# Decays of the later blocks by two scans on 96 partitions, factor products moved ahead of the first value products, x of pair 1 moved to the weights' queue, and units reordered around the value products of pair 1

**Chip, cores, metric.** One core of a Trainium2 chip. The metric is the device time of one execution in microseconds (us). A profiled run has a span a little shorter than its time (128.0 for 129.73 us). "State" is fast or slow: a run more than 1.5% above the fastest of the same kernel counts as slow. Comparisons of times below use fast runs.

## The reference

A state-space scan (batch 4, 8 heads, 768 steps, head size 32, state size 16), then a bilinear layer with two weights of 256x1536 and one of 1536x256:

```python
for c in range(nc):                       # chunks of the sequence
    L = np.exp(cum[:, :, :, None] - cum[:, :, None, :]) * causal
    M = np.einsum('bhin,bhjn->bhij', Cc, Bc) * L
    y[:, :, sl] = np.einsum('bhij,bhjd->bhid', M, xc) + y_inter   # y_inter from state and C
    state = decay_full * state + np.sum(Bx, axis=2)
...
x = attn_out.transpose(0, 2, 1, 3).reshape(B * S, H * D)
return (x @ w_a) * (x @ w_b) @ w_out
```

## The kernel before

The kernel takes blocks of 128 steps, and each block in two pairs of batches: 12 pairs, numbered 0 to 11. For a pair, B and C are multiplied by factors from the running products of `a` (bm, cm), transposed on TensorE, and multiplied with each other (`scores`). The scores are masked and multiplied with x (`pv`, the value products). Six `unit`s then form the bilinear product hk of the pair, and two `out_half`s the output. TensorE has enough to do from pair 2 on; the head of the program, where everything first has to arrive, is what the change is about. Cuts are marked.

```python
    nc.sync.dma_start(a_sb, a.rearrange("b h (k q) -> (b h) k q", q=Q))      # 32 partitions
    # ... B, C, x of pair 0 by ScalarE and SyncE; B and C of pair 1 by SyncE
    load1(nc.sync, 1, 2, 0)               # x of pair 1
    load1(nc.sync, 1, 2, 1)
    load(2)
    # ... GpSimd: selections; load_w(0); causal
    load_w(1, (0,))                       # Wa chunk 1 (Wb chunk 1 follows behind the masks of pair 0)

    def scan(lo, hi):
        for k in range(lo, hi):
            nc.vector.tensor_tensor_scan(Pr[:, k], a_sb[:, k], zero, 1.0, ALU.mult, ALU.add)
    # ...
    scan(0, 1); sel_over_mid(0, 1); v = factors_mm(0, 1)
    # ... factors, bm and cm of pair 0 on DVE, scan(1, 2), transposes(0), scan(2, 3), scores(0), masks
    load_w(1, (1,))                       # Wb chunk 1
    load_w(2)
    scale_bc(1, 1, nc.gpsimd)             # cm, bm of pair 1
    scale_bc(1, 0, nc.gpsimd)
    # ... value products of pair 0
    scan(3, NBLK)
    h = unit(0, 0)
    turn(0)
    sel_over_mid(1, NBLK)
    h()
    go((0, 1))
    v = factors_mm(1, NBLK)               # 40 matmuls
    # ... hr, hs, hsx on DVE
    transposes(1, None, nc.vector.tensor_copy)
    nc.scalar.copy(flat(fC, 1, NBLK), v)
    h = unit(0, 2)
    fb(1)
    scores(1)                             # start: mark S of the prediction
    # ... masks of pair 1, unit (0, 3), G matmul
    go((0, 4))
    pv(1)                                 # start: mark P
    state(0)
    state(1)
    go((0, 5), (1, 0), (1, 1), (1, 2))
    transposes(2)
    go((1, 3))
    # ... scores(2), units (1, 4), (1, 5), out_half(0, 0), pv(2), out_half(0, 1)
    transposes(3)
```

## Time and profile before

| | before |
|---|---|
| time, median of the first 3 runs | 131.09 us (130.17 to 131.13) |
| span, mean granted clock of the profiled run | 128.0 us, 0.999 |
| TensorE busy | 93% |

The prediction shows the page's rows, the windows, the waits and the chain of this kernel. Two views more are needed later. The view of transfers (destination and source, queue, size, median time from issue to landing):

```profile
a_sb<-in_a_dram SPq DMA_DIRECT2D x1, 96.0 KB, 2.1
cn<-in_C_dram ACTq DMA_DIRECT2D x1, 64.0 KB, 3.2
```

All decays arrived in 2.1 us, and the first half of C of pair 0 in 3.2. And TensorE's timeline (start, duration, line, operation, and in brackets the idle time before it with what ended it):

```profile
10.82 0.80 PE L476 MATMUL aps<-X2T,Wa 128*128 128x256 f16 x4
...
13.21 1.38 PE L225 MATMUL fps<-selr,Pr 32*64 32x16 f32 x40
...
31.51 0.28 PE L313 MATMUL SC<-ident,bm 128*128 128x128 f16 x2
```

Unit (0,0) starts at 10.82, the 40 factor matmuls stand on the path at 13.21, and the transposes of pair 3 start at 31.51. From there on TensorE is full, so the start of that last line, called T3 below, says what the head costs.

### The profile page before, as it was taken

What the parts mean: (1) busy time and instruction counts of PE and PEld (TensorE: products, weight loads), DVE (VectorE), ACT (ScalarE), POOL (GpSimd) and SP (SyncE); (2) the same over time, 40 slices, a digit from 0 to 9 for tenths busy, and PEclk for the clock granted to TensorE, in tenths of its full rate; (3) what the DMA queues carried; (4) which work ended last, traced back from release to release, by engine and by line L of the source; (5) the groups of instructions that cost most, each with busy time, mean ns of one, the idle gap of its engine ahead of it and who ended that gap; (6) DMA issues with size and microseconds to landing.
All of it is one profiled execution on the core that took longest, in us unless ns stands there. A gap on an engine that the chain in (4) does not pass through costs nothing.

```text
span 128.0 us, 4399 instructions
## 1 busy us (share of the span) xinstructions
PE 118.6 (93%) x1761; PEld 97.1 (76%) x1761; DVE 89.6 (70%) x178; ACT 66.5 (52%) x129; POOL 62.0 (48%) x106
## 2 busy tenths in 40 slices
PE   6969979799999999999999999999999999999960
PEld 2425757688887888888888888888888888888840
DVE  4676769658695976967958959959759569364420
ACT  3344567594836545455556456465445464564410
POOL 7966830799982925907828447338339100000000
PEclk9999999999999999999999999999999999999999
DMA  3999999775435666566456555565565310211203
GB/s 66 158 215 164 211 199 216 117 136 111 105 67 88 156 90 111 120 110 142 91 96 146 104 87 131 111 111 123 101 133 116 73 42 0 46 41 23 51 8 82
DMA packets 51555, 13.76 MB, mean 107 GB/s; under 512 B 45328, under 2 KB 51504, under 8 KB 51536
## 3 DMA queue, kind: packets, MB, share of 16 engines
q1 hardware_dynamic: 46560, 10.72, 43.8%
q0 software_dynamic: 3184, 2.36, 12.5%
q10 hardware_dynamic: 1792, 0.41, 1.6%
q8 instruction: 13, 0.21, 0.7%
q14 instruction: 6, 0.05, 0.1%
HBM read 11.13 MB, written 3.15 MB: 111 GB/s over the span
## 4 chain that ended last, share of the span: by engine, by line
PE 77%; DMA 9%; SPq 7%; POOL 1%; issue 1%; ACTq 1%; DVE 0%; POOLq 0%
PE ops L493 25%; PE aps L476 22%; PE bps L476 21%; DMA cn<-in_C_dram 9%; SPq L123 7%; PE SC L380 3%; PE SC L336 3%; PE SC L397 2%; ACTq L123 1%; POOL bm L262 1%; PE SC L313 0%; POOL cm L262 0%; DVE osb L506 0%; POOLq L451 0%; POOLq L262 0%
## 5 line engine op out<-in xcount | busy, mean ns | idle before, releaser
L486 DVE TENSOR_TENSOR hk<-bps,asb 128x512 f16<-128x512 f32 x72 | 49.2, 687 | 20.8 <-ACT asb L485 18.9
L485 ACT COPY asb<-aps 128x512 f32<-128x512 f32 x72 | 42.1, 587 | 17.9 <-PE aps L476 16.4
L476 PE MATMUL bps<-X2T,Wb 128*128 128x256 f16 x288 | 43.2, 273 | 1.1 <-ACT G L611 1.1
L476 PE MATMUL aps<-X2T,Wa 128*128 128x256 f16 x288 | 43.5, 273 | 0.1
L493 PE MATMUL ops<-Wo,hk 128*128 128x256 f16 x288 | 35.3, 273 | 0.0
L476 PEld LDWEIGHTS <-Wb 128*128 128x128 f16 x288 | 28.1, 98 | 4.5 <-issue 0.6
L493 PEld LDWEIGHTS <-hk 128*128 128x128 f16 x288 | 27.4, 98 | 4.1
L476 PEld LDWEIGHTS <-Wa 128*128 128x128 f16 x288 | 26.8, 98 | 4.8 <-issue 0.3
L370 DVE TENSOR_TENSOR t<-SC,causal 128x512 f16<-128x512 f32 x45 | 29.4, 681 | 1.3 <-ACT tmp L367 1.0
L451 POOL TENSOR_TENSOR sbd<-U,maskbd 128x512 f16<-128x512 f32 x10 | 11.5, 1154 | 21.1 <-DVE U L447 21.0
L508 ACT ACTIVATE osb<-ops 128x256 f32<-128x256 f32 x23 | 8.8, 383 | 23.6 <-PE ops L493 22.9
L249 POOL TENSOR_SCALAR x<-xn 128x512 f16<-128x512 f32 x9 | 13.4, 1489 | 0.8 <-DMA xn<-in_x_dram 0.2
L408 ACT ACTIVATE X2T<-SC 128x512 f16<-128x512 f32 x11 | 6.6, 597 | 5.1 <-PE SC L380 5.1
L262 POOL TENSOR_TENSOR bc<-cn,fC 128x128 f16<-128x128 f32 x16 | 6.1, 402 | 5.6 <-DMA cn<-in_C_dram 3.4
L262 POOL TENSOR_TENSOR t<-bn,fB 128x256 f16<-128x256 f32 x12 | 7.7, 639 | 0.1
L262 POOL TENSOR_TENSOR bc<-bn,fB 128x128 f16<-128x128 f32 x16 | 6.1, 401 | 0.0
L380 PEld LDWEIGHTS <-x 64*32 64x32 f16 x384 | 3.2, 91 | 3.2 <-ACT x L247 1.6
L201 PE MATMUL SC<-warm 128*128 128x512 f16 (+1 forms) x14 | 4.4, 453 | 1.2 <-DVE warm L150 1.2
L427 DVE STREAM_TRANSPOSE dt<-SC 128x64 f32<-128x64 f32 x9 | 2.2, 249 | 4.1 <-ACT X2T L408 4.1
L262 POOL TENSOR_TENSOR cm<-cn,fC 128x128 f16<-128x128 f32 (+1 forms) x5 | 2.1, 445 | 5.9 <-DMA cn<-in_C_dram 5.9
L368 POOL TENSOR_TENSOR t<-tmp,causal 128x512 f16<-128x512 f32 x3 | 3.5, 1156 | 3.1 <-ACT tmp L367 3.1
L380 PE MATMUL SC<-t,x 64*32 64x144 f16 (+1 forms) x352 | 4.8, 224 | 0.0
(69 smaller groups left out, 66.8 us busy)
## 6 DMA issues: line engine op xcount, KB each, us to landing
xn<-in_x_dram SPq DMA_DIRECT2D x23, 128.0 KB, 3.2
out_dram<-osb SPq DMA_DIRECT2D x46, 64.0 KB, 2.1
bn<-in_B_dram SPq DMA_DIRECT2D x23, 64.0 KB, 2.7
cn<-in_C_dram SPq DMA_DIRECT2D x23, 64.0 KB, 3.3
Wa<-in_moe_w_a_dram POOLq DMA_DIRECT2D x3, 256.0 KB, 6.8
Wb<-in_moe_w_b_dram POOLq DMA_DIRECT2D x3, 256.0 KB, 6.6
Wo<-in_moe_w_out_dram POOLq DMA_DIRECT2D x1, 768.0 KB, 10.2
xn<-in_x_dram ACTq DMA_DIRECT2D x1, 128.0 KB, 5.4
```

Source lines behind the costliest of these rows:

```text
L123: return eng.dma_start(pair_in[p][which][64 * bt : 64 * bt + 64].rearrange("i h r n -> i h (r n)"), src.rearrange("h (i r) n -> i h (r n)" ...
L249: eng.tensor_scalar(xo, xi, XS, None, ALU.mult)
L262: return eng.tensor_tensor(out=out, in0=i0, in1=i1, op=ALU.mult)
L370: nc.vector.tensor_tensor(out=o_, in0=i_, in1=c_, op=ALU.mult)
L380: nc.tensor.matmul(py[bt][32 * g : 32 * g + 32, u * (Q + N) : u * (Q + N) + w], s["X16"][k, h, r, :], s["T1"][k, h, r, 0:w], start=(first ...
L408: nc.scalar.activation(out=X2T[:, p].rearrange("p u t q -> p t u q"), in_=s["PY"][:, :, :, 0:Q], func=AF.Copy, scale=YS / XS,)
L451: nc.gpsimd.tensor_tensor(out=Sbd.rearrange("p t (h d) -> p t h d", h=H), in0=U32[:, p].unsqueeze(2).broadcast_to((128, 2, H, D)), in1=mas ...
L476: nc.tensor.matmul(ps[:, kk * 2 * Q : (kk + 1) * 2 * Q], W[:, f, k * 128 : (k + 1) * 128], X2T[:, p, f].rearrange("p t q -> p (t q)"), sta ...
L485: nc.scalar.copy(asb, a_ps)
L486: return lambda: nc.vector.tensor_tensor(out=s["hk"][:, 2 * k2 : 2 * k2 + 2, :].rearrange("p k q -> p (k q)"), in0=b_ps, in1=asb, op=ALU.mult)
L493: nc.tensor.matmul(o_ps[:, 0:d_model], hk[:, k, bt * Q : (bt + 1) * Q], Wo[:, k, :], start=(k == 0), stop=(k == NK - 1), skip_group_check= ...
L508: nc.scalar.activation(out=o_sb, in_=o_ps[:, 0:d_model], func=AF.Copy, scale=1.0 / (YS * YS))
```

## The change

The intent: scan block 0 alone from a small load, so that the head starts early; bring the other decays to 96 partitions (32 rows of batch and head, times three thirds of the sequence), so that two scans replace five; do the factor matmuls in TensorE's idle time before the first value products; leave SyncE's queue to B and C by giving x of pair 1 to GpSimd's; and reorder the units around the value products of pair 1.

```diff
-    nc.sync.dma_start(a_sb, a.rearrange("b h (k q) -> (b h) k q", q=Q))
+    nc.sync.dma_start(a0_sb, a.rearrange("b h s -> (b h) s")[:, 0:Q])
+    nc.gpsimd.dma_start(a_sb.rearrange("p t q -> p (t q)"), a.rearrange("b h (k c) -> k (b h) c", k=KP))
...
-    load1(nc.sync, 1, 2, 0)
-    load1(nc.sync, 1, 2, 1)
     load(2)
...
     load_w(0)
...
-    load_w(1, (0,))
+    load_w(1)
...
+    for t in range(2):
+        scan(Pr[:, t], a_sb[:, t])
+    nc.vector.reciprocal(rmid, Pr[:, :, 63])
...
     scores(0)
+    load1(nc.gpsimd, 1, 2, 0)
     n0 = tail(0, nc.gpsimd)
+    for t in range(2):
+        over_mid(nc.gpsimd, selr[:, t].rearrange("p k b t h -> p (k b t h)"), rmid[:, t : t + 1])
...
-    load_w(1, (1,))
+    load1(nc.gpsimd, 1, 2, 1)
     load_w(2)
-    scale_bc(1, 1, nc.gpsimd)
     scale_bc(1, 0, nc.gpsimd)
...
-    warmup(5, tcp)
...
+    warmup(1, tcp)
+    for t in range(2):
+        factors_mm([F[:, :, t, r] for r in range(2)], Pr[:, t], [selr[:, t, :, :, bt] for bt in range(2)])
+    nc.scalar.copy(flat(fC, 1, NBLK), fps[:, 2 * NBP * H : NBLK * 2 * NBP * H])
+    warmup(1, tcp)
...
     h = unit(0, 0)
     turn(0)
-    sel_over_mid(1, NBLK)
     h()
+    scale_bc(1, 1, nc.vector)
     go((0, 1))
-    v = factors_mm(1, NBLK)
...
-    go((0, 4))
     pv(1)
+    turn(1)
+    go((1, 0))
+    gps = bank("gps")          # the G matmul, on 96 rows
...
-    go((0, 5), (1, 0), (1, 1), (1, 2))
+    go((1, 2), (1, 3))
     transposes(2)
-    go((1, 3))
-    h = unit(1, 4)
+    go((0, 4))
+    h = unit(0, 5)
...
```

More of the change, by code (lines that the diff above doesn't have):

```diff
@@ L52 @@
     NG = NBLK - 1
+    KP = NBLK // 2
+    KR = KP * BH
     j = np.arange(128)
-    bh = np.arange(BH)
-    p32 = np.zeros((BH, 128 + nb * NG), np.float32)
-    p32[:, 0:128] = (bh[:, None] % H) == (j // N % 2 * (H // 2) + j // (2 * N))[None, :]
+    row = np.arange(KR)
+    p96 = np.zeros((KR, 128 + nb * KP), np.float32)
+    p96[:, 0:128] = (row[:, None] % H) == (j // N % 2 * (H // 2) + j // (2 * N))[None, :]
     for b in range(nb):
-        p32[b * H : (b + 1) * H, 128 + b * NG : 128 + (b + 1) * NG] = 1.0
-    p32_t = nc.inline_tensor(p32, "p32")
+        for k in range(KP):
+            p96[k * BH + b * H : k * BH + (b + 1) * H, 128 + b * KP + k] = 1.0
+    p96_t = nc.inline_tensor(p96, "p96")
     const = ctx.enter_context(tc.tile_pool(name="const", bufs=1))
-    c32 = const.tile([BH, p32.shape[1]], f32, name="c32")
+    c96 = const.tile([KR, p96.shape[1]], f32, name="c96")
     headm = const.tile([128, H], f32, name="headm")
@@ L68 @@
     causal = const.tile([128, 2, Q], f16, name="causal")
-    sel = const.tile([BH, 2, NBP, H], f32, name="sel")
-    indm = c32[:, 0:128]
-    selb = c32[:, 128 : 128 + nb * NG]
+    indm = c96[:, 0:128]
+    selb = c96[:, 128 : 128 + nb * KP]
     big = ctx.enter_context(tc.tile_pool(name="big", bufs=1))
-    a_sb = big.tile([BH, NBLK, Q], f32, name="a_sb")
-    zero = big.tile([BH, Q], f32, name="zero")
+    a_sb = big.tile([KR, 2, Q], f32, name="a_sb")
+    a0_sb = big.tile([BH, Q], f32, name="a0_sb")
+    zero = big.tile([KR, Q], f32, name="zero")
+    Pr0 = big.tile([BH, Q], f32, name="Pr0")
+    rmid0 = big.tile([BH, 1], f32, name="rmid0")
+    selr0 = big.tile([BH, NBP, 2, H], f32, name="selr0")
     Wa = big.tile([128, 2, d_ff], f16, name="Wa")
@@ L83 @@
     warm = big.tile([128, 512], f16, name="warm")
-    Pr = big.tile([BH, NBLK, Q], f32, name="Pr")
-    rmid = big.tile([BH, NBLK], f32, name="rmid")
-    selr = big.tile([BH, NBLK, 2, NBP * H], f32, name="selr")
+    Pr = big.tile([KR, 2, Q], f32, name="Pr")
+    rmid = big.tile([KR, 2], f32, name="rmid")
+    selr = big.tile([KR, 2, KP, NBP, 2, H], f32, name="selr")
     fB = big.tile([128, NBLK, 2, NBP, H], f32, name="fB")
     fC = big.tile([128, NBLK, 2, NBP, H], f32, name="fC")
-    hr = big.tile([BH, NG], f32, name="hr")
-    hs = big.tile([BH, NG], f32, name="hs")
-    hsx = big.tile([BH, nb, NG], f32, name="hsx")
-    G = big.tile([128, nb, NG], f32, name="G")
+    nxt = big.tile([KR, 2], f32, name="nxt")
+    hr = big.tile([KR, 2], f32, name="hr")
+    hs = big.tile([KR, 2], f32, name="hs")
+    hsx = big.tile([KR, nb, KP, 2], f32, name="hsx")
+    G = big.tile([128, nb, NBLK], f32, name="G")
     bc = [big.tile([128, 6, H, N], f16, name=f"bc{i}") for i in range(2)]
@@ L140 @@
     load1(nc.scalar, 0, 2, 1)
-    nc.scalar.dma_start(c32, p32_t.ap())
+    nc.scalar.dma_start(c96, p96_t.ap())
     load1(nc.sync, 0, 2, 0)
@@ L146 @@
     load1(nc.sync, 1, 1, 0)
-    load1(nc.sync, 1, 2, 0)
-    load1(nc.sync, 1, 2, 1)
     load(2)
     nc.vector.memset(warm.bitcast(u32), 0)
+    nc.vector.memset(ident, 1.0)
+    nc.vector.memset(headm, 1.0)
     nc.vector.memset(zero, 0.0)
-    for t_ in bc:
-        nc.vector.memset(t_[:, 0:4].rearrange("p k h n -> p (k h n)").bitcast(u32), 0)
-    nc.gpsimd.memset(sel, 1.0)
+    nc.vector.memset(causal, 1.0)
     nc.gpsimd.affine_select(
-        out=sel,
-        in_=sel,
-        compare_op=ALU.is_equal,
-        fill=0.0,
-        base=0,
-        pattern=[[-H, 2], [-2 * H, NBP], [-1, H]],
-        channel_multiplier=1,
+        out=ident, in_=ident, compare_op=ALU.is_equal, fill=0.0, base=0, pattern=[[-1, 128]], channel_multiplier=1
     )
-    nc.gpsimd.memset(headm, 1.0)
     for sign, base in ((1, 0), (-1, N - 1)):
@@ L177 @@
     )
-    nc.gpsimd.memset(ident, 1.0)
-    nc.gpsimd.affine_select(
-        out=ident, in_=ident, compare_op=ALU.is_equal, fill=0.0, base=0, pattern=[[-1, 128]], channel_multiplier=1
-    )
     KC = 4 * 128
@@ L190 @@
     load_w(0)
-    nc.gpsimd.memset(causal, 1.0)
     for bt in range(2):
@@ L203, in warmup, with scan, over_mid, factors_mm @@
             )
-    def scan(lo, hi):
-        for k in range(lo, hi):
-            nc.vector.tensor_tensor_scan(Pr[:, k], a_sb[:, k], zero, 1.0, ALU.mult, ALU.add)
-    def sel_over_mid(lo, hi):
-        nc.vector.reciprocal(rmid[:, lo:hi], Pr[:, lo:hi, 63])
-        nc.vector.tensor_tensor(
-            out=selr[:, lo:hi].rearrange("p k t c -> p k (t c)"),
-            in0=sel.rearrange("p t b h -> p (t b h)").unsqueeze(1).broadcast_to((BH, hi - lo, 2 * NBP * H)),
-            in1=rmid[:, lo:hi].unsqueeze(2).broadcast_to((BH, hi - lo, 2 * NBP * H)),
-            op=ALU.mult,
-        )
-    def factors_mm(lo, hi):
-        fps = psf.tile([128, 512], f32, name="fps", tag="ff")
-        F = fps[:, 0 : (hi - lo) * 2 * NBP * H].rearrange("p (k r c) -> p k r c", k=hi - lo, r=2)
-        for k in range(lo, hi):
-            for r in range(2):
-                for bt in range(2):
-                    nc.tensor.matmul(
-                        F[64 * bt : 64 * bt + 64, k - lo, r],
-                        Pr[:, k].rearrange("p (i r) -> p r i", r=2)[:, r],
-                        selr[:, k, bt],
-                        start=True,
-                        stop=True,
-                        skip_group_check=True,
-                        tile_position=(0, 64 * bt),
-                    )
-        return F.rearrange("p k r c -> p (k r c)")
+    def scan(pr, a_):
+        nc.vector.tensor_tensor_scan(pr, a_, zero[0 : pr.shape[0]], 1.0, ALU.mult, ALU.add)
+    def over_mid(eng, sr, rm):
+        n = rm.shape[0]
+        eng.tensor_scalar(sr, ident[0:n, 0:n], rm, None, ALU.mult)
+    def factors_mm(F, pr, sr):
+        for r in range(2):
+            for bt in range(2):
+                nc.tensor.matmul(
+                    F[r][64 * bt : 64 * bt + 64],
+                    pr.rearrange("p (i r) -> p r i", r=2)[:, r],
+                    sr[bt],
+                    start=True,
+                    stop=True,
+                    skip_group_check=True,
+                    tile_position=(0, 64 * bt),
+                )
     def flat(f, lo, hi):
@@ L535 @@
     warmup(1, SC[3], 128)
-    scan(0, 1)
-    sel_over_mid(0, 1)
-    v = factors_mm(0, 1)
+    scan(Pr0, a0_sb)
+    nc.vector.reciprocal(rmid0, Pr0[:, 63:64])
+    over_mid(nc.vector, selr0.rearrange("p b t h -> p (b t h)"), rmid0)
+    v = bank("fps")[:, 0 : 2 * NBP * H]
+    v5 = v.rearrange("p (r b h) -> p r b h", r=2, b=NBP)
+    factors_mm([v5[:, r] for r in range(2)], Pr0, [selr0[:, :, bt] for bt in range(2)])
     nc.vector.reciprocal(flat(fB, 0, 1), v)
@@ L544 @@
     n1 = scale_bc(0, 1, nc.vector)
-    scan(1, 2)
     tb, tcp = bank("tb"), bank("tc")
-    transposes(0, [tb, tcp], nc.vector.tensor_copy, lambda: warmup(2, SC[3], 128))
-    scan(2, 3)
+    transposes(0, [tb, tcp], None, lambda: warmup(2, SC[3], 128))
+    for t in range(2):
+        scan(Pr[:, t], a_sb[:, t])
+    nc.vector.reciprocal(rmid, Pr[:, :, 63])
     warmup(1, SC[3])
@@ L565 @@
     nc.gpsimd.tensor_copy(maskbd, headm.unsqueeze(2).broadcast_to((128, H, D)))
+    for t_ in bc:
+        nc.gpsimd.memset(t_[:, 0:4].rearrange("p k h n -> p (k h n)").bitcast(u32), 0)
     n0 = load(3)
     tc.add_manual_dep(n0[0].ins, wd[5].ins.name, AFTER, reason="weights first")
-    warmup(5, tcp)
+    fps = bank("fps")
+    F = fps[:, 0 : NBLK * 2 * NBP * H].rearrange("p (k t r b h) -> p k t r b h", k=KP, t=2, r=2, b=NBP)
+    warmup(1, tcp)
[3 more added lines that the diff above has]
+    warmup(1, tcp)
     py = st[0]["py"] = [bank("py0"), bank("py1")]
@@ L579 @@
     warmup(1, tcp, 128)
-    scan(3, NBLK)
     h = unit(0, 0)
     turn(0)
-    sel_over_mid(1, NBLK)
     h()
+    scale_bc(1, 1, nc.vector)
     go((0, 1))
-    v = factors_mm(1, NBLK)
-    nc.vector.tensor_tensor(out=hr, in0=Pr[:, 0:NG, Q - 1], in1=rmid[:, 0:NG], op=ALU.mult)
-    nc.vector.tensor_tensor(out=hs, in0=hr, in1=Pr[:, 1:NBLK, 63], op=ALU.mult)
-    nc.vector.tensor_tensor(
-        out=hsx,
-        in0=hs.unsqueeze(1).broadcast_to((BH, nb, NG)),
-        in1=selb.rearrange("p (b g) -> p b g", b=nb),
-        op=ALU.mult,
-    )
     transposes(1, None, nc.vector.tensor_copy)
-    nc.scalar.copy(flat(fC, 1, NBLK), v)
     h = unit(0, 2)
@@ L606 @@
     load(4)
-    gps = bank("gps")
-    nc.tensor.matmul(
-        gps[:, 0 : nb * NG], indm, hsx.rearrange("p b g -> p (b g)"), start=True, stop=True, skip_group_check=True
-    )
-    nc.scalar.copy(G.rearrange("p b g -> p (b g)"), gps[:, 0 : nb * NG])
     mask(product(1, 1))
     h()
+    nc.gpsimd.memset(nxt, 0.0)
+    nc.gpsimd.tensor_copy(nxt[:, 0:1], Pr[:, 1, 63:64])
+    for k in range(KP - 1):
+        nc.gpsimd.tensor_copy(nxt[k * BH : (k + 1) * BH, 1:2], Pr[(k + 1) * BH : (k + 2) * BH, 0, 63:64])
+    nc.gpsimd.tensor_tensor(out=hr, in0=Pr[:, :, Q - 1], in1=rmid, op=ALU.mult)
+    nc.gpsimd.tensor_tensor(out=hs, in0=hr, in1=nxt, op=ALU.mult)
+    nc.gpsimd.tensor_tensor(
+        out=hsx,
+        in0=hs.unsqueeze(1).unsqueeze(1).broadcast_to((KR, nb, KP, 2)),
+        in1=selb.rearrange("p (b k) -> p b k", b=nb).unsqueeze(3).broadcast_to((KR, nb, KP, 2)),
+        op=ALU.mult,
+    )
     scale_bc(2, 1, nc.gpsimd)
@@ L616 @@
     tail(2, nc.gpsimd)
-    go((0, 4))
     pv(1)
+    turn(1)
+    go((1, 0))
+    gps = bank("gps")
+    nc.tensor.matmul(
+        gps[:, 0 : nb * NBLK], indm, hsx.rearrange("p b k t -> p (b k t)"), start=True, stop=True, skip_group_check=True
+    )
+    nc.scalar.copy(G.rearrange("p b g -> p (b g)"), gps[:, 0 : nb * NBLK])
+    go((1, 1))
     state(0)
     state(1)
-    go((0, 5), (1, 0), (1, 1), (1, 2))
+    go((1, 2), (1, 3))
     transposes(2)
-    go((1, 3))
-    h = unit(1, 4)
+    go((0, 4))
+    h = unit(0, 5)
     scores(2)
@@ L628 @@
     scale_x(2, nc.scalar)
-    h2 = unit(1, 5)
+    h2 = unit(1, 4)
     mask(product(2, 1))
+    h()
     mask(product(2, 2))
-    h()
+    h2()
+    go((1, 5))
     out_half(0, 0)
-    h2()
     scale(3)
```

## The prediction

> **What bounds the kernel now.** I read the page from the top. The engine row shows TensorE full for nearly the whole span, and the chain of work that ended last agrees.
>
> ```profile
> PE 118.6 (93%) x1761; PEld 97.1 (76%) x1761; DVE 89.6 (70%) x178; ACT 66.5 (52%) x129; POOL 62.0 (48%) x106
> PE   6969979799999999999999999999999999999960
> PEclk9999999999999999999999999999999999999999
> PE 77%; DMA 9%; SPq 7%; POOL 1%; issue 1%; ACTq 1%; DVE 0%; POOLq 0%
> ```
>
> One digit is 3.2 us, so from the eighth on TensorE never waits, at full clock. Only the first 25 us hold anything to win. Cutting that stretch at its events, the view by windows (PE is the first busy column, the last two are DMA share and GB/s) says:
>
> ```profile
> 13.20:14.52 1.32, 1.31 (x42) 1.29 (x41) 1.32 (x3) 0.19 (x1) 1.32 (x3) 1.00 1.23 207
> 14.52:16.17 1.65, 1.27 (x16) 1.02 (x13) 0.74 (x5) 1.22 (x4) 1.06 (x2) 1.00 1.30 216
> 16.17:20.05 3.88, 2.82 (x52) 1.97 (x51) 2.90 (x6) 2.54 (x6) 1.15 (x1) 1.00 1.40 198
> 20.05:24.86 4.81, 4.04 (x65) 3.30 (x65) 4.05 (x11) 2.89 (x5) 1.54 (x5) 1.00 1.20 177
> 24.86:31.40 6.54, 6.54 (x120) 5.51 (x121) 4.44 (x9) 4.64 (x10) 6.48 (x11) 1.00 0.62 116
> ```
>
> The first of these windows is work that the change moves: the 40 factor matmuls. The other holes are 0.38, 1.06 and 0.77 us, all in a stretch where the DMA engines are more than full. From 24.86 there is no hole. The view of waits, for 10.8 to 31.4 us, names the holes, and the chain view shows the last:
>
> ```profile
> POOL cm L262 <- DMA cn<-in_C_dram: 5.9, 2, 4.8
> PE bps L476 <- ACT G L611: 1.1, 1, 1.1
> DVE t L370 <- ACT tmp L367: 1.0, 1, 1.0
> PE SC L313 <- POOL bm L262: 0.8, 1, 0.8
> PEld L476 <- DMA Wb<-in_moe_w_b_dram: 0.6, 1, 0.6
> PE SC L336 <- DVE ct L323: 0.4, 1, 0.4
> ```
> ```profile
> 14.54 8.65 DMA cn<-in_C_dram
> 23.68 0.40 POOL cm L262
> 24.09 0.73 POOL bm L262 x2
> 24.86 0.23 PE SC L313
> ```
>
> The C rows of pair 2, issued at 14.54, land at 23.19, and the transposes of pair 2 wait for them. I use two marks: **S**, where the scores of pair 1 start (16.17), and **P**, where the value products of pair 1 start (20.05). Between them runs a chain that is not TensorE's:
>
> ```profile
> 16.74 0.59 ACT L367 COPY tmp<-SC 128x512 f32<-128x512 f32 x1 [0.28 <-PE SC L336]
> 17.36 0.69 DVE L370 TENSOR_TENSOR t<-SC,causal 128x512 f16<-128x512 f32 x1 [0.98 <-ACT tmp L367]
> 17.97 0.68 DVE L486 TENSOR_TENSOR hk<-bps,asb 128x512 f16<-128x512 f32 x1
> 18.57 1.28 DVE L370 TENSOR_TENSOR t<-SC,causal 128x512 f16<-128x512 f32 x2
> ```
>
> The last mask ends at 19.85 and P follows at 20.05. So the 1.06 us wait for Wb in unit (0,4) lies beside this chain: without it TensorE would have stood idle before P instead. It is worth almost nothing.
>
> **What the Trainium skill says.** "DMA: Bandwidth & Descriptors", section "Issuing engines are not separate DMA queues": transfers of all issuers run on the same 16 engines and interleave; another issuer saves only sequencer time. The trace agrees: about 200 GB/s at a share of 1.2 to 1.4 whoever issues, so moving x of pair 1 to GpSimd's queue reorders arrivals and brings no bandwidth. "GPSIMD Engine Reference", section 3 (Performance versus the Vector engine): both engines take 128 lanes at once and GpSimd is about 2 times slower at two inputs. In the trace a mask takes 1156 ns on POOL and 681 on DVE; by the lanes I expect a 96-partition scan to cost what one of 32 costs (0.41 us). "TensorE: Matmul & The Clock Gate", Part 1: an idle window of some 3.4 us halves the clock. Before has no such idle, so this trace can't test it; I return to it below.
>
> **The change, part by part.**
> *Scans.* Before: six on DVE (3 in the head, then 3 taking 1.03 us from 10.98). After: one for block 0, then two on 96 partitions, about 0.82 us, done in the head. The three at 10.98 delayed the turn of pair 0, and with sel_over_mid (0.13 + 0.75) the first hk product, from about 12.27 to 12.99. DVE also loses hr, hs and hsx (0.40 + 0.16 + 0.17).
> *Factor products.* 40 matmuls, 1.31 us on TensorE's path, become 8 with three times the columns, between the scores of pair 0 and its value products, where 5 warmups (1.25 us) stood. At 0.1 us each (an estimate, three times the 33 ns of before) they take 0.8 us after GpSimd has made selr. I put that at 8.5 us: a_sb issue 0.9, two issues and the selects as before, Wa and Wb 1.5, x 0.8, tail 0.63, two small products 0.6. Value products started at 9.40 after x16 (9.35), so this just fits, and X2T of pair 0 still comes at about 10.8.
> *In the head* ct of pair 0 goes to ScalarE behind two bt copies (to 6.72, plus 0.37), so its scores move from 6.56 to about 7.15 and DVE's masks end at 9.7 instead of 9.1. The second value products began at 10.03: hidden.
> *cm of pair 1* goes from POOL to DVE: 12.95 to 13.38 behind the first hk product. Unit (0,1) ends at 12.8, C transposes start at about 13.4, unit (0,2) at 13.6. ScalarE's bt ends at about 14.05, ct at 14.4, so **S is 14.5** at best. Unit (0,2) stands before the scores and needs the second Wb chunk, which landed at 14.9 when issued at 8.96. Issued some 3 us earlier but behind a_sb in a FIFO ring, I expect it at 14.0 to 14.6: S is 14.5 to 15.0, that is 1.2 to 1.7 us earlier.
> *S to P* keeps the chain above, the same instructions in the same order: 3.88 us. P becomes 18.4 to 18.9. But units (0,4) and (0,5) and the G matmul have moved behind P. Of TensorE's work only unit (0,3), 0.87 us, is left beside the chain: it will stand idle some 2.6 us there.
> *P to the transposes of pair 3* (31.40 before, 11.35 us after P). Less the wait for bm of pair 2 (0.77, and with the drain of the matmul before it 0.93) this is 10.42 of issue. After adds unit (0,4) 0.87 and G 0.35. It adds a wait of 0.85, as (1,0) stands right behind P and needs X2T of pair 1 (ScalarE's copy ended 1.12 after P; before, (0,5) filled this). The bm wait goes, as C of pair 2 moves two transfers ahead: the transfers two places earlier landed at 19.0 to 19.2, so bm is done by 20.7 and is wanted at P + 5.1. A new one comes: output half (0,0) now needs hk of (0,5), which DVE makes after two masks of pair 2, and (1,5) needs ScalarE's copy for (1,4), behind tmp and x16; both at about P + 10 when TensorE is there at P + 9.3. Together 10.42 + 0.87 + 0.35 + 0.85 + 0.8 = 13.3.
> *Sum.* Transposes of pair 3 at 14.5 + 3.9 + 13.3 = 31.7, or 32.2 with S at 15.0, against 31.40. Behind them TensorE is full in both, so the shift stays: plus 0.3 to 0.8. Each added wait was taken whole, and a little less traffic ahead of x of pair 0 may bring its start 0.1 to 0.3 forward. I settle at plus 0.1: **131.2 us**.
>
> **The rivals.**
> 1. *It gains what was meant*: factor products 1.31, bm wait 0.93 and the Wb wait 1.06 all vanish, 3.3 us, and the time is about 127.8. For it: each is a hole or path work in the trace. Against it: the S to P chain holds P, and TensorE has too little to do before it. A half gain, 129.3, needs the waits for X2T and at output half (0,0) to be hidden after all.
> 2. *The weights become the bound*: x in their queue and a_sb ahead of them make Wb chunk 1 late (15.5), unit (0,2) waits, S is hardly earlier, and the later order costs its 2 us: 133. For it: the share of 1.2 to 1.4. Against it: Wb chunk 1 is issued earlier.
> 3. *The clock*: around P TensorE works only some 0.4 us of 3.8. If that counts as idle, the next 3.4 us run at half rate, 1.7 us more. Against it: the page asks for a whole idle window, and its phase is free.
>
> **Range and chances.** The parts cancel: 1.2 to 1.7 won up to S, some 2 lost behind P, each good to 0.5. With the spread of the runs before (130.17 to 131.13) the range is 129.5 to 132.6. Faster by over 2% needs 2.6 us, nearly all of rival 1: 0.1. Slower by over 2% needs rivals 2 and 3: 0.04. Within 2%: 0.86.
>
> **What would show it.** In the profile after: no factor matmul between units (0,1) and (0,2); S at 14.5 to 15.0; P 3.9 later; TensorE idle over 2 us before P and some 0.8 behind it; no wait for bm at the transposes of pair 2; a wait of 0.5 to 1 us before output half (0,0); transposes of pair 3 at 31.4 to 32.2. I am wrong if P comes before 18 us, if the holes around P are small, or if a weight lands late enough to hold a unit for over 1 us.

## The result

135.44 us (median of 4, 134.64 to 135.64) against 130.63 us (4 runs, 129.8 to 131.13) for the kernel before: the ratio is 1.0363, 95% interval 1.0286 to 1.0441. Ratios here and below are the mean time of one kernel's fast runs over that of the other's of the same rounds, so not quite the ratio of the medians. The predicted 131.2 and the range up to 132.6 were wrong: the change costs about 5 us. The profiled run of the changed kernel has a span of 133.9 us. Its page:

```profile
PE 120.8 (90%) x1734; PEld 98.0 (73%) x1734; DVE 89.1 (67%) x172; ACT 66.9 (50%) x130; POOL 65.4 (49%) x114
...
PEclk9975799779999999999999999999999999999999
```

The clock row is the first thing that is new: two dips. In the trace's clock records TensorE ran at half rate from 8.23 to 15.05 us and from 25.29 to 28.71; before, it had full clock from 5.0 to the end. TensorE's timeline:

```profile
10.79 1.10 PE L211 MATMUL fps<-selr,Pr 96*64 96x48 f32 x16
...
14.26 0.99 PE L461 MATMUL aps<-X2T,Wa 128*128 128x256 f16 x4
...
17.21 0.28 PE L298 MATMUL SC<-ident,bm 128*128 128x128 f16 x2 [0.65 <-POOL bm L247]
18.09 0.28 PE L298 MATMUL SC<-ident,cm 128*128 128x128 f16 x2 [0.60 <-DVE cm L247]
...
19.63 0.43 PE L321 MATMUL SC<-ct,bt 32*64 32x128 f16 x32 [0.38 <-DVE ct L308]
...
23.32 0.43 PE L365 MATMUL SC<-t,x 64*32 64x144 f16 x28 [0.26 <-DVE t L355]
24.46 0.60 PE L461 MATMUL aps<-X2T,Wa 128*128 128x256 f16 x4 [0.71 <-ACT X2T L393]
...
37.77 0.28 PE L298 MATMUL SC<-ident,bm 128*128 128x128 f16 x2
```

The factor matmuls did go ahead of the value products, but at 10.79 and not at 8.5, and unit (0,0) is at 14.26 instead of 10.82. What TensorE waited for is in the view of waits (total, times, longest) and in the view of transfers:

```profile
PE tc L298 <- DVE cm L247: 2.5, 1, 2.5
...
DVE cm L247 <- DMA cn<-in_C_dram: 3.0, 2, 2.4
...
POOL bm L247 <- DMA bn<-in_B_dram: 2.1, 1, 2.1
```
```profile
a_sb<-in_a_dram POOLq DMA_DIRECT2D x1, 96.0 KB, 5.8
...
cn<-in_C_dram ACTq DMA_DIRECT2D x1, 64.0 KB, 6.2
```

The 96 KB of decays, 2.1 us before, take 5.8 us, and C of pair 0, issued at the same time in both kernels, 6.2 us instead of 3.2. The chain of work that ended last now passes through C twice (start, length):

```profile
1.56 6.16 DMA cn<-in_C_dram
...
7.74 9.28 DMA cn<-in_C_dram
```

Split at the prediction's marks, in us. S is the start of the scores of pair 1, P that of their value products (the large group of matmuls, where they come in two):

| stage | before | after | difference |
|---|---|---|---|
| start of unit (0,0) | 10.82 | 14.26 | +3.44 |
| unit (0,0) to S | 5.35 | 5.37 | +0.02 |
| S to P | 3.88 | 3.69 | -0.19 |
| P to T3 | 11.46 | 14.45 | +2.99 |
| T3 | 31.51 | 37.77 | +6.26 |

So three questions: what made the head 3.4 us late, why removing 1.3 us of factor matmuls between unit (0,0) and S gained nothing, and what of the 3.0 us behind P is order and what is clock.

### The profile page after: what moved, and what is told of

Read it like the earlier page. It is cut to its first block, busy times and chain, and to the rows that moved or that the text cites. A ratio compares the mean times of both kernels' runs of the same rounds, so it can differ in the third digit from the quotient of the medians.

```text
span 133.9 us, 4347 instructions
## 1 busy us (share of the span) xinstructions
PE 120.8 (90%) x1734; PEld 98.0 (73%) x1734; DVE 89.1 (67%) x172; ACT 66.9 (50%) x130; POOL 65.4 (49%) x114
## 3 DMA queue, kind: packets, MB, share of 16 engines
HBM read 11.18 MB, written 3.15 MB: 107 GB/s over the span
## 4 chain that ended last, share of the span: by engine, by line
PE 75%; DMA 12%; DVE 5%; ACT 3%; issue 2%; ACTq 1%; DVEq 0%
PE ops L478 24%; PE aps L461 21%; PE bps L461 21%; DMA cn<-in_C_dram 12%; PE SC L365 3%; PE SC L321 3%; DVE hk L471 2%; PE SC L382 2%; DVE t L355 1%; ACT asb L470 1%; DVE cm L247 1%; ACT bt L307 1%; DVE U L430 1%; ACTq L131 1%; ACT x L232 0%
## 5 line engine op out<-in xcount | busy, mean ns | idle before, releaser
L461 PE MATMUL aps<-X2T,Wa 128*128 128x256 f16 x288 | 44.6, 279 | 0.7 <-ACT X2T L393 0.7
L461 PE MATMUL bps<-X2T,Wb 128*128 128x256 f16 x288 | 44.0, 276 | 0.4 <-ACT asb L470 0.4
L461 PEld LDWEIGHTS <-Wb 128*128 128x128 f16 x288 | 28.7, 99 | 4.3 <-issue 0.5
L461 PEld LDWEIGHTS <-Wa 128*128 128x128 f16 x288 | 27.7, 100 | 5.5 <-issue 1.0
L196 PEld LDWEIGHTS <-warm 128*128 128x128 f16 x20 | 2.0, 121 | 3.5 <-issue 2.0
```

The source lines that it names most:

```text
L196: nc.tensor.matmul(bank[:, 0:cols], warm[:, 0:128], warm[:, 0:cols], start=True, stop=True, skip_group_check=True)
L461: nc.tensor.matmul(ps[:, kk * 2 * Q : (kk + 1) * 2 * Q], W[:, f, k * 128 : (k + 1) * 128], X2T[:, p, f].rearrange("p t q -> p (t q)"), sta ...
```

## The experiments

Theory at first: the large load of `a` in GpSimd's queue delays what follows. Rival: the queues' new order (weights, x) does it. All diffs are against the changed kernel ("after") unless they say "before". Every run was also profiled. Times are medians, this kernel / the kernel before of the same call.

**e1: the load of `a` issued by ScalarE instead of GpSimd.**

```diff
-    nc.gpsimd.dma_start(a_sb..., a.rearrange("b h (k c) -> k (b h) c", k=KP))
     load1(nc.scalar, 0, 1, 1)
+    nc.scalar.dma_start(a_sb..., a.rearrange("b h (k c) -> k (b h) c", k=KP))
```

> The changed kernel with one edit: the 96-partition load of a is issued by ScalarE (after the C load) instead of by GpSimd as its first transfer. Theory A (that load, first in GpSimd's queue, holds some of the 16 DMA engines for about 3 us, so C and x of pair 0 land late): C of pair 0 lands near 5.2 to 5.8 us instead of 8.2, unit (0,0) starts near 11 instead of 14.3, and the time falls by 3 to 5 us, to 130.5 to 132.5. Rival B (the deeper weight queue, with x of pair 1 and the second Wb chunk early, starves the other loads): C of pair 0 stays near 8 us and the time stays near 135.

136.82 / 130.26, ratio 1.0514 [1.0452, 1.0576]: worse. It is not GpSimd's queue.

**e2: the queues of before** (x of pair 1 back in SyncE's queue, Wb chunk 1 back behind the masks).

```diff
+    load1(nc.sync, 1, 2, 0)
+    load1(nc.sync, 1, 2, 1)
     load(2)
-    load_w(1)
+    load_w(1, (0,))
-    load1(nc.gpsimd, 1, 2, 0)
-    load1(nc.gpsimd, 1, 2, 1)
+    load_w(1, (1,))
     load_w(2)
```

> The changed kernel with x of pair 1 back in SyncE's queue and the second Wb chunk issued late, as before; the load of a stays first in GpSimd's queue. Theory A: unit (0,0) still starts near 14 us, the time stays within 1 us of the changed kernel's (134.5 to 136). Rival B: unit (0,0) near 11 us, the time near 131.

136.03 / 130.26, ratio 1.044 [1.037, 1.0509]. The second half of C of pair 0 still landed at 8.03 us (before 5.19), and unit (0,0) started at 14.07. The queues' order does not make the head late.

**e3: the kernel before, plus the same load into a tile that nobody reads.**

```diff
+    a_96 = big.tile([96, 2, Q], f32, name="a_96")
+    nc.gpsimd.dma_start(a_96.rearrange("p t q -> p (t q)"), a.rearrange("b h (k c) -> k (b h) c", k=3))
     tiles(0)
```

> The kernel before with one addition: the same 96-partition load of a, into a tile that nothing reads, as GpSimd's first transfer. Theory A: C of pair 0 lands 2 to 3 us later, unit (0,0) starts 2 to 3.5 us later, and the time rises by 2.5 to 5 us, to 133.5 to 136. Rival B: within 0.7 us of the kernel before.

134.09 / 130.26, ratio 1.0294 [1.0197, 1.0391]. One unread transfer of 96 KB alone costs the kernel before 3%; C of pair 0 landed at 8.07. A transfer's semaphore is raised 16 times in the trace, once for each DMA engine, and the 16 times tell what is wrong with this one (us, in order):

```
load of a, e3:            first 4.07   8th 4.38   12th 4.48   14th 6.93   15th 7.31   16th 7.32
C of pair 0 (SyncE), e3:  first 4.64   8th 5.05   12th 5.30   14th 7.66   15th 8.01   16th 8.07
C of pair 0, before:      first 4.34   8th 4.62   12th 4.99   14th 5.02   15th 5.14   16th 5.19
```

Thirteen engines are done by 4.49, three need until 7.32, and everything that is spread over all 16 and comes behind waits for these three. The source is read as `k (b h) c`, so its slowest dimension has 3 entries. The Trainium skill, "DMA: Bandwidth & Descriptors", section "Why a DMA increments its semaphore by 16 and not by 1", says that a transfer runs on the largest number of engines, up to 16, that divides the slowest dimension of both sides, and that for a transfer issued by GpSimd all 16 engines raise the semaphore, whatever its shape. For slowest dimensions of 3 and 96 that is 3 engines. The increments agree (the page names an exception for some of GpSimd's copies; it did not apply to this one).

**e6: e3 with one word of it changed**: the same bytes in the order `(b h k) c`, whose slowest dimension is 96.

```diff
-    a.rearrange("b h (k c) -> k (b h) c", k=3)
+    a.rearrange("b h (k c) -> (b h k) c", k=3)
```

> As the earlier addition to the kernel before (a load of a into an unread 96-partition tile, first in GpSimd's queue), but with the rows taken in the order in which they lie in memory, so that the source's outermost size is 96 in place of 3. Same bytes, same 1 KB rows, one issue. Theory A2: runs on 16 engines, C of pair 0 lands at 5 to 5.7 us, the time within 0.8 us of the kernel before. Rival A1: about 3 to 4 us above it, as the earlier addition.

130.94 / 130.14, ratio 1.0063 [1.0029, 1.0097]. All 16 increments now fall between 3.50 and 4.25, and C of pair 0 lands at 5.59. From the views of transfers, e3 and then e6:

```profile
a<-in_a_dram POOLq DMA_DIRECT2D x1, 96.0 KB, 5.9
```
```profile
a<-in_a_dram POOLq DMA_DIRECT2D x1, 96.0 KB, 2.9
```

The same bytes, queue and issuer: 3.0 us less, and of the 3% that the load cost only 0.6% is left. With this pair of runs the cause of the late C of pair 0 is shown, not only argued; how much of the late head it is, e9 below tells.

**e5 and e8: the load in three parts of 32 partitions** (slowest dimension 32), issued by GpSimd (e5) or by ScalarE behind x of pair 0 (e8).

```diff
-    nc.gpsimd.dma_start(a_sb..., a.rearrange("b h (k c) -> k (b h) c", k=KP))
+    for k in range(KP):
+        nc.gpsimd.dma_start(a_sb[k * BH : (k + 1) * BH]..., a.rearrange("b h s -> (b h) s")[:, k * 2 * Q : (k + 1) * 2 * Q])
```

> The changed kernel with its 96-partition load of a cut into three loads of 32 partitions, in the same place of GpSimd's queue, same bytes. Theory A2 (the one load runs on only 3 of the 16 DMA engines, as its source's outermost size is 3; they fall 3 us behind and every later load, spread over all 16, waits for them): all 16 increments of each part come together, C of pair 0 lands at 5 to 6 us, unit (0,0) starts at 10.8 to 11.5, the scores of pair 1 at 14.5 to 16, and the time is 130.5 to 132.5 (the value first predicted, plus a possible half-clock stretch of 1.6 us around the value products of pair 1). Rival A1 (any load of these bytes ahead of the weights does this): C of pair 0 still near 8 us, the time stays near 135.

> The three parts issued by ScalarE behind x of pair 0, so that GpSimd starts the weights at once. If GpSimd's 2 us of issuing held the weights (second Wb chunk) back, this is up to 1 us under the three-part version on GpSimd; if not, the two are equal within 0.5 us, or this is up to 1 us slower because the scans wait for a later a. 130 to 132.5.

e5: 134.35 / 130.14, ratio 1.0324 [1.027, 1.0378]. C of pair 0 came at 6.55, but unit (0,0) only at 13.24: less than I expected. What now held the factor matmuls until 9.69 was GpSimd's own chain: three issues (1.76 us in all), the weights' issues, x's issue (0.73), tail (0.64) and two products for selr (0.52 each). DVE's small reduction `par` also waited for GpSimd's selections behind the three issues and held the first scan up until 4.03, but cm of pair 0 (6.67) waited for C in any case. And this head ran at half clock: e5's clock records show full clock only from 15.44. e8: 137.97 / 130.14, ratio 1.059 [1.0553, 1.0626]. ScalarE stood in the three issues for 3.96 us and its first copy came late, so this is no cure:

```profile
ACT fC L532 <- DMA a_sb<-in_a_dram: 6.0, 1, 6.0
```

**e4 and e7: nine warm-up matmuls behind unit (0,3)**, on the changed kernel and on e5, to fill the hole before P.

```diff
     mask(product(1, 1))
     h()
+    warmup(9, bank("wg"))
     nc.gpsimd.memset(nxt, 0.0)
```

> The changed kernel with nine 512-column warm-up matmuls (about 1.9 us at full clock) put into TensorE's idle time before the value products of pair 1. If the second stretch at half clock (25.3 to 28.7 us) comes from that idle time and costs what its matmuls lost, it is gone and the time falls by 1.2 to 1.8 us, to 133.7 to 134.3. If the clock follows something else, the stretch stays and the time is the changed kernel's within 0.5 us.

> The three-part load together with the nine warm-up matmuls in TensorE's idle time before the value products of pair 1. If the idle time there halves the clock also when the head is early, this is 1 to 1.8 us under the three-part version alone; if the free-running window does not catch it, the two are equal within 0.5 us. Either way 129.5 to 131.5.

e4: 134.28 / 130.26, ratio 1.0316 [1.0258, 1.0375], only 0.5 points under the changed kernel's, which was measured in another call; e7: 132.8 / 130.14, ratio 1.0205 [1.0168, 1.0241], 1.5 us under e5 in the same call. In e4's clock records the second dip is gone (full clock from 17.3 to the end), and P to T3 falls from 14.45 to 13.47 us; in e7, from e5's 14.83 to 13.46. So of the +3.0 us behind P some 1.0 to 1.4 is the halved clock, and 2.0 (13.47 against 11.46) is the order.

**e9: the changed kernel with the load in one issue on 16 engines.** The rows are then in the wrong order, so the output is wrong on purpose (relative error 0.138); the instructions and the bytes are the same.

```diff
-    a.rearrange("b h (k c) -> k (b h) c", k=KP)
+    a.rearrange("b h (k c) -> (b h k) c", k=KP)
```

**e10: e9, with selr made by DVE and `par` behind the first scan. e11: e10 with the warm-ups of e4.**

```diff
-        over_mid(nc.gpsimd, selr[:, t]...)
+        over_mid(nc.vector, selr[:, t]...)
...
-    nc.vector.tensor_reduce(out=par, ...)      # ahead of the first scan
+    nc.vector.tensor_reduce(out=par, ...)      # behind it
```

> The changed kernel with one character group moved: the 96-partition load reads the rows in the order in which they lie, so it is one issue of the same bytes over 16 DMA engines; the decays then belong to the wrong rows and the result is wrong on purpose. Theory A2 alone: C of pair 0 lands at 5.2 to 6 us, and with it goes the head's delay, unit (0,0) at 10.8 to 11.2, time 130.5 to 132. Theory B2 (beside the 3-engine load the head has new serial steps, above all GpSimd's x issue, tail and two selr products of 0.5 us ahead of the factor products): C early, but unit (0,0) only at 11.6 to 12.3, time 131.5 to 133.5.

> The same (wrong on purpose), and the two selr products on VectorE in place of GpSimd and par after the first scan in place of ahead of it. Theory B2: unit (0,0) 0.7 to 1.3 us earlier than in the version with the 16-engine load alone, at 10.8 to 11.4, and the time 0.7 to 1.5 us lower, 130.3 to 132. Theory A2 alone: no difference over 0.4 us.

> The same, and nine warm-up matmuls in TensorE's idle time before the value products of pair 1. If the half clock is caught there, 1 to 1.8 us under the version without them: 129.5 to 131. If the window misses the idle time, equal within 0.5 us.

e9: 134.37 / 129.73, ratio 1.0349 [1.0236, 1.0462]. e10: 134.32, of which two fast runs at 132.81 and 133.74; ratio 1.0288 [1.0164, 1.0411]. e11: 135.3, with one fast run only (132.17), so no ratio. The profiled runs of e10 and e11 were in the slow state. Unit (0,0) starts at 14.26, 12.27 and 10.92 in after, e9 and e10. After and e9 both ran at half clock from the factor matmuls to unit (0,0) (3.47 and 3.56 us), so the 2.0 us between them are the load. e9 and e10, however, differ in the clock as well: the records show full clock only from 13.31 in e9, and from 5.21 in e10 (a warm-up matmul of 512 columns takes 0.61 us in e9 and in after, 0.39 in e10). The factor matmuls and unit (0,0), e9 and then e10:

```profile
8.71 1.18 PE L211 MATMUL fps<-selr,Pr 96*64 96x48 f32 x16 [0.29 <-POOL selr L206]
...
12.27 1.06 PE L461 MATMUL aps<-X2T,Wa 128*128 128x256 f16 x4
```
```profile
7.96 0.69 PE L208 MATMUL fps<-selr,Pr 96*64 96x48 f32 x16
...
10.92 0.80 PE L458 MATMUL aps<-X2T,Wa 128*128 128x256 f16 x4
```

The factor matmuls start 0.75 us earlier, and the stretch from there to unit (0,0) is 0.6 shorter, 2.96 us. `par` has no part in this: DVE's bm of pair 0 starts at 5.08 in both. So **the head's 3.44 us are 2.0 of the three-engine load, 0.75 of selr on GpSimd, and about 0.6 of a stretch at half clock**, which the kernel before did not have there; what caused that stretch in e9 is not shown. But the gain did not reach the time. In e9 the unit work ran dry behind unit (0,1):

```profile
POOL bm L247 <- DMA bn<-in_B_dram: 2.6, 1, 2.6
```

B and C of pair 1 landed at 14.98 and 15.52 in e9 and at 14.52 and 17.01 in e10; before, at 11.77 and 12.13.

**e12: the kernel before, with x of pair 1 in GpSimd's queue** and nothing else.

```diff
-    load1(nc.sync, 1, 2, 0)
-    load1(nc.sync, 1, 2, 1)
...
     scores(0)
+    load1(nc.gpsimd, 1, 2, 0)
...
+    load1(nc.gpsimd, 1, 2, 1)
     load_w(1, (1,))
```

> The kernel before with one part of the change alone: x of pair 1 in GpSimd's weight queue. C of pair 2 then lands 2 us or more before 23.2, the 0.77 us wait for bm before the transposes of pair 2 goes, and the time falls by 0.3 to 0.9 us. If x or the third weight chunk comes late instead, it rises by up to 1 us.

130.4 / 129.73, ratio 1.0086 [1.0002, 1.0171]: this part alone gains nothing. B and C of pair 1 landed at 12.84 and 13.18, a microsecond later than before, although they are issued ahead of it by another engine, and Wb chunk 1, now behind x, held TensorE up:

```profile
PEld L474 <- DMA Wb<-in_moe_w_b_dram: 1.2, 1, 1.2
```

**e13, e14, e15: e10 with the queues of before** (the diff of e2); with Wb chunk 1 alone moved back (e14); and e13 with the warm-ups of e4 (e15). The output is wrong on purpose again.

> Wrong output on purpose, as in the run before with the head on DVE (e10), to which one thing is added: x of pair 1 back in SyncE's queue and Wb chunk 1 back behind the masks of pair 0. Queue theory (the early Wb chunk 1 and x of pair 1, between the weights and B and C of pair 1, are what made these land at 14.5 and 17.0): B of pair 1 lands by 12.6, C by 13.3, the scores of pair 1 start at 14.5 to 15.5 (e10: over 17), P 3.8 later, transposes of pair 3 at 31.7 to 33, and the time is 0.99 to 1.01 of the kernel before, 1.5% more if a half-rate clock window still falls behind P. Rival (the slow state of that profile, or the other new traffic, made them late): B and C land at 14 or later as in e10 and the time stays at 1.03.

> Wrong output on purpose. As e13, but x of pair 1 stays in GpSimd's queue, so only Wb chunk 1 moves back. If Wb chunk 1 is what delays B and C of pair 1: as e13 within 0.5 us, B and C by 13.3. If x in GpSimd's queue is: they land as in e10 (14.5, 17.0). From e12, where x alone was moved in the kernel before and B and C came 1 us later, I expect about 1 us later than e13.

> Wrong output on purpose. e13 with 9 warm-up matmuls behind unit (0,3), which fill the hole before P. If e13 shows a half-rate clock window behind P, this one shows none there and is 1.2 to 1.6 us shorter; if e13 has none, the two agree within 0.4 us.

e13: 133.36 / 130.36, ratio 1.0232 [1.0182, 1.0283]. e14: 134.4, ratio 1.0358 [1.0299, 1.0418]. e15: 131.87, ratio 1.0102 [1.0044, 1.016]. B and C of pair 1 landed at 12.42 and 13.31 in e13 and at 13.49 and 13.91 in e14: both parts of the new queue order delay them, x in GpSimd's queue by 1.1 and 0.6 us (e14 to e13), Wb chunk 1 by 1.0 and 3.1 (e10 to e14; a slow run against a fast one, so these two are rough). My expectation for S was missed, though: 16.09, not 14.5 to 15.5. e13's timeline names what held it:

```profile
15.45 0.72 PE L460 MATMUL bps<-X2T,Wb 128*128 128x256 f16 x4 [0.67 <-DMA Wb<-in_moe_w_b_dram]
16.09 0.65 PE L320 MATMUL SC<-ct,bt 32*64 32x128 f16 x32
```

Unit (0,2) needs Wb chunk 1 and stands ahead of the scores. Whichever of B, C and Wb chunk 1 goes first, the last of them comes no earlier than before (14.87; in e9, e13 and e14 15.52, 15.40 and 17.14). That answers the second question: the factor matmuls had stood in time that the transfers took anyway. e15 against e13 gives the clock's price once more, 1.5 us, and its P to T3 is 13.56 us, at full clock throughout.

**e16: right output, every repair at once.** The three parts of e5 issued behind GpSimd's selections, DVE's steps as in e10, queues as in e13, and the units' order of before around P.

```diff
-    pv(1); turn(1); go((1, 0))
+    go((0, 4)); pv(1); turn(1); go((0, 5))
...
-    go((1, 1)); state(0); state(1); go((1, 2), (1, 3)); transposes(2); go((0, 4)); h = unit(0, 5)
+    state(0); state(1); go((1, 0), (1, 1), (1, 2)); transposes(2); go((1, 3)); h = unit(1, 4)
```

> Right output. The changed kernel with every repair at once: the load of a in three parts of 32 partitions (16 engines each) issued behind GpSimd's selects, selr and par on DVE as in e10, queues as in e13, and units (0,4) and (0,5) back in the places of the kernel before (before P and right behind it). If the order behind P was the rest of the loss: scores of pair 1 at 14.5 to 15.5, P at 18.4 to 19.4, no hole over 1.8 us before P, transposes of pair 3 at P + 11.4, that is 29.8 to 30.8 (before 31.4), and the time 0.985 to 0.995 of the kernel before. Rival: the three issues make the first weights late, unit (0,0) starts at 11.5 or later instead of 10.8, and the time is 1.00 or above.

130.89 / 130.36, ratio 1.0058 [1.0012, 1.0103]. Its rival came true: the third part of `a` landed at 8.06, the clock fell, and unit (0,0) started at 13.56. Yet it is 3 points faster than the changed kernel, chiefly since P to T3 fell to 11.18 us. From e15, which has the same queues and full clock behind P as well, it differs there in the order of the units. P and T3 in e15 and then in e16:

```profile
20.09 0.43 PE L364 MATMUL SC<-t,x 64*32 64x144 f16 x28 [0.17 <-DVE t L354]
...
33.65 0.28 PE L297 MATMUL SC<-ident,bm 128*128 128x128 f16 x2
```
```profile
21.88 0.43 PE L368 MATMUL SC<-t,x 64*32 64x144 f16 x28 [0.26 <-DVE t L358]
...
33.06 0.28 PE L301 MATMUL SC<-ident,bm 128*128 128x128 f16 x2
```

So **the order costs 2.4 us** (13.56 against 11.18). Against the kernel before it is 2.0 to 2.1, as that one had the wait of 0.77 us for bm of pair 2 inside its 11.46.

**e17: right output, one issue on 16 engines, and unit (0,2) behind the scores of pair 1.** The rows stay in the order `(b h k)` of the load, and the selections, the product's output and the constants follow it. The one step that then crosses partitions is a transfer of 4 bytes for each of 95 rows. Otherwise as e16.

```diff
+    nc.sync.dma_start(nxt[0 : KR - 1, 1:2], Pr[1:KR, 0, 63:64])
+    load(2)
...
-    factors_mm([F[:, :, t, r] for r in range(2)], Pr[:, t], [selr[:, t, :, :, bt] for bt in range(2)])
+    factors_mm([F[:, :, t, r].rearrange("p k b h -> p b h k") for r in range(2)], Pr[:, t], [selr[:, t, :, bt] for bt in range(2)])
...
-    h = unit(0, 2)
     fb(1)
     scores(1)
     mask(product(1, 3), by_pool=True)
+    h = unit(0, 2)
```

> Right output. The load of a in one issue and on 16 engines, its rows ordered by batch, head and third of the sequence (the selections, the product's output and the one step over the row's end, a small transfer, follow); selr and par on DVE, queues as in e13, units (0,4) and (0,5) as in the kernel before, and one thing more: unit (0,2), which waited for Wb chunk 1 until 15.45 in e13 and held the scores of pair 1 behind it, stands behind these scores. If Wb chunk 1 is what holds S once the head is repaired: unit (0,0) at 10.6 to 11.2, S at 14.7 to 15.2 (e13: 16.09), P at 18.6 to 19.1, transposes of pair 3 at P + 11.4, that is 30.0 to 30.5 (before 31.4), and the time 0.985 to 0.995 of the kernel before. Rival: B and C of pair 1 or the mask on GpSimd hold it, and the time stays at 1.00 to 1.01.

**e18: the kernel before, with that move of unit (0,2) alone** (the last five lines of the diff above).

> Right output. The kernel before with that one move alone: unit (0,2) behind the scores of pair 1 instead of ahead of them. If units ahead of S are path and units between S and P are free, S comes about 0.9 earlier (15.2 instead of 16.17), P at 19.1, transposes of pair 3 at 30.5, and the time is 0.990 to 0.996 of before. Rival: the scores wait for their transposes' copies (ct at 15 or so) or P for the masks behind a later asb, and the time is 0.997 to 1.003.

e17: 129.1 / 130.1, ratio 0.9958 [0.989, 1.0027]; e18: 130.42 / 130.1, ratio 1.008 [1.0018, 1.0141]. e17's timeline:

```profile
10.80 0.80 PE L460 MATMUL aps<-X2T,Wa 128*128 128x256 f16 x4
...
14.99 0.43 PE L320 MATMUL SC<-ct,bt 32*64 32x128 f16 x32 [1.25 <-DVE ct L307]
...
18.78 1.03 PE L460 MATMUL bps<-X2T,Wb 128*128 128x256 f16 x4
19.74 0.44 PE L364 MATMUL SC<-t,x 64*32 64x144 f16 x32
...
30.63 0.28 PE L297 MATMUL SC<-ident,bm 128*128 128x128 f16 x2
```

Unit (0,0) and S are where the prediction had put them for the changed kernel (10.8; 14.5 to 15.0), 1.2 us before S of the kernel before. P did not follow, because the hole of 1.25 us before S was followed by 3.4 us of half clock: a unit's four matmuls take 1.03 us at 18.78 instead of 0.60, and in the view by windows TensorE is busy for all of S to P, while the last mask ended at 18.62 (busy time is the second number, the granted clock the third from the end):

```profile
14.99:19.74 4.75, 4.75 (x56) 3.32 (x56) 3.28 (x6) 2.77 (x5) 2.69 (x8) 0.64 1.47 199
```

T3 is 30.63, against 31.51 before. e18's S came at 16.02 only, waiting for the copy of C's transposes, which had started behind the factor matmuls at 14.37: the move is worth nothing while these stand in the path. Its P came at 21.10, with a half-clock stretch from 16.89 to 20.31 in between, so its time does not measure the move alone. e17 recovers the whole loss of the changed kernel; that it beats the kernel before is not established, as the interval includes 1.

| kernel | unit (0,0) | S | P | T3 | ratio to before |
|---|---|---|---|---|---|
| before | 10.82 | 16.17 | 20.05 | 31.51 | 1 |
| after | 14.26 | 19.63 | 23.32 | 37.77 | 1.0363 |
| e9 | 12.27 | 17.64 | 21.32 | 35.77 | 1.0349 |
| e13 | 10.64 | 16.09 | 19.97 | 35.27 | 1.0232 |
| e15 | 11.22 | 16.41 | 20.09 | 33.65 | 1.0102 |
| e16 | 13.56 | 18.20 | 21.88 | 33.06 | 1.0058 |
| e17 | 10.80 | 14.99 | 19.74 | 30.63 | 0.9958 |

The marks are those of one profiled run each; the ratios are of all fast runs, and differ from the marks by up to 1.2 per cent. The granted clock differs from run to run, which may be why (e9's profiled run was 133.64 us, its runs went to 135.48).

## Why the prediction was wrong

- **The load of `a` was the step that failed first.** The prediction counted it as "a_sb issue 0.9", an issue and no transfer, and closed with "a little less traffic ahead of x of pair 0 may bring its start 0.1 to 0.3 forward". Measured: 5.8 us instead of 2.1, C of pair 0 3 us late. The sum of bytes was the same; their spread over the engines was not. e3 against e6 shows it.
- **selr and the factor matmuls: nearly right without the load, but at half clock.** "I put that at 8.5 us" used 0.6 us for two small products on GpSimd; they took 0.52 each. With the load on 16 engines (e9) the matmuls started at 8.71, with selr on DVE (e10) at 7.96. But from there to unit (0,0) the prediction's 2.3 us became 3.56 at half clock in e9, and 2.96 at full clock in e10. That `par` now stood in DVE's order ahead of the first scan was not seen; in the changed kernel it held this scan until 3.32 (e10: 2.44), hidden behind the late C. The two scans on 96 partitions took 0.73 us in e9 and e10, where 0.82 was said.
- **Unit (0,0) to S.** The prediction took 1.2 to 1.7 us off here and made Wb chunk 1 alone responsible, "at 14.0 to 14.6". It assumed that B and C of pair 1 would arrive as before. They came 4.7 and 4.9 us later in the changed kernel (with the load on 16 engines, e9, still 3.2 and 3.4), and with the old queue order Wb chunk 1 held S at 16.09 (e13). Rival 2 had the right place and named the wrong tensors. With both out of the way (e17) S was 14.99, the predicted figure; e13, with the factor matmuls moved but not unit (0,2), and e18, with the unit moved but not the matmuls, have 16.09 and 16.02.
- **S to P: right.** 3.69 against 3.88, with 2.0 us of idle TensorE before P (1.77 ahead of a first group of four matmuls and 0.26 behind it) where 2.6 was said.
- **P to T3: right in its sum, apart from the clock.** Predicted 13.3, measured 13.47 to 13.56 at full clock (e4, e7, e15). The wait for X2T was 0.71 (0.85 predicted), the wait for bm of pair 2 was gone as predicted, the wait before output half (0,0) was 0.36 (0.8 predicted); at full clock (e4) there were two in its place, 0.36 and 0.35. So the reordering of units was a loss by itself, as the prediction's arithmetic said and its intent did not.
- **The clock.** Rival 3 had the mechanism and its size (1.7 us; 1.5 by e15 and e7), but got almost no weight. It happened in the changed kernel twice. The argument against it, that a whole idle window is needed, did not hold: see the last section.
- **One line was misread, without effect.** The prediction calls the 1.06 us before the second half of unit (0,4) a wait for Wb. The view it shows names ScalarE's copy of G: this copy ended at 19.47, behind the scaling of x of pair 1 (x came at 18.69), while Wb's chunk was there at 18.75. The conclusion, that the wait lies beside the mask chain, stands.

The sum of the miss at T3: +3.4 in the head, where nothing was expected; 1.2 to 1.7 not gained before S; 1.0 to 1.4 of clock behind P. Only the +2 behind P had been in the sum.

## What to carry to other kernels

When a load is rewritten to another partition layout, look at the slowest dimension of both access patterns before counting bytes: 96 rows read as 3 x 32 ran on 3 engines, slowed every transfer behind it, and a reordering of the rows removed this. When work is taken off the path in a stretch where the DMA engines are full, ask which transfer the next step waits for; here removal alone gained nothing, and only with the unit that waited for a weight behind the scores did S move. A hole made in TensorE's work costs its own length and may cost another 1.5 us of halved clock.

## What the Trainium skill lacked or had wrong

- "TensorE: Matmul & The Clock Gate", Part 1: it gives at least one idle window of some 3.4 us as the condition for half rate. The runs agree on the quantum (half-rate stretches of 3.413 and 6.827 us), but not on idleness: in the 3.41 us ahead of the switch TensorE was busy for 1.03 and 1.51 us in the changed kernel, 1.90 us in e17 and 2.16 us in e18, the last with its longest hole at 1.25 us. In the changed kernel two earlier windows with 2.16 and 2.20 us of work kept full clock, and e15 kept it through a window with 2.04 while e12 lost it after one with 2.32, so the busy share alone is not the criterion; what is stays open. The page's section "A second HAM failure mode: psum-queue depth-cycling" does say that short idle times between groups of matmuls can make the clock oscillate, but gives no measure of them.
- "DMA: Bandwidth & Descriptors", the section on the 16 increments: right on the number of engines, but no word there of what a transfer on few engines does to those behind it. In e3 the 3 engines finished 2.4 to 2.8 us after the other 13, and the transfers behind, on all 16 engines, ended about as much later (C of pair 0 at 8.07 instead of 5.19).
